# GEGLU feed-forward on one core: one down product of the first group as two row tiles of 64

## The chip, the cores and the metric

The kernel runs on one core of a Trainium2 chip. The metric is the device time of one execution in microseconds. All times in this text are microseconds (us) unless marked ns. The engines are called PE (matrix multiply; PEld is its weight load), DVE (vector), ACT (scalar), POOL and SP (here only a queue that issues transfers).

## What is computed

```python
def reference(x, w_gate, w_up, w_down):
    return (_gelu(x @ w_gate) * (x @ w_up)) @ w_down
```

x is 2048 x 1024, w_gate and w_up are 1024 x 3584, w_down is 3584 x 1024, all bf16; `_gelu` is the tanh form. The change lies in the last product, by w_down.

## The kernel before

The 2048 rows of x are taken in two halves of 1024 (`h`). For each half the hidden activations `hT` (3584 features on partitions, 28 blocks of 128, by 1024 rows) are made first, in `pair_quads`; then two calls of `down_group` multiply them by w_down, 512 rows each (`grp` 0 and 1). The run of the program is thus: hidden for half 0, down groups 0 and 1, hidden for half 1, down groups 2 and 3. `n` numbers the four groups; the change is in group 0, which runs from 183 to 227 us of the profiled span.

A down group is one 2 x 2 block product in Strassen's form as Winograd has it, with seven products in place of eight. The 28 blocks of features are split into two halves of 14 (`NS`), the 512 rows into two halves of 256 and the 1024 output columns into two halves of 512 (`DN`). The seven products are called m1, m5, m6, m7, m2, m3 and m4, in the order in which they run. Each is a sum over 14 blocks `i` of 128 features, for two sets `u` of 128 rows: 28 matmuls of 128 x 128 (weights) by 128 x 512 (moving), which add up in two PSUM banks, one for each `u`. m1 and m2 have bf16 operands. The other five have sums and differences of blocks as operands, held in fp32r (4 bytes): the left ones (`s1` to `s4`, `a22`) in `s_mem`, made by `s_down`, mostly on DVE; the right ones (`t1` to `t4`, `b22`) in `t_mem`, made by `t_down`: t1 and t3 on DVE, b22 by a cast on ACT, t2 and t4 by a transfer on SP from `t_dram`, where an earlier stage put them. The profile shows fp32r matmuls as f32.

`t_mem` is a ring of 20 slots (`NR`) for operands of 14 blocks each, so the next operand's first six blocks are made ahead, and its blocks 6 to 13 go into slots that the present product has read. `s_mem` has two places for a left operand; s1, s2 and s4 share the first, a22 and s3 the second. Hence work is put behind a product's matmuls: the argument `behind` of `product` is called after each odd `i`, and what it emits waits for that matmul. For m3 (left operand s4, right operand b22, banks 4 and 5, called QB) that is `behind_m3`: after i = 1, 3, 5 and 7 a transfer of two blocks of t4, which m4 reads from its seventh block on; after each odd i two blocks of s1 of the next group on DVE; and after i = 9, 11 and 13 two blocks of t1 of the next group on DVE. m4 runs in the order `tail`: i = 0 to 8 with both u in turn, then i = 9 to 13 for u = 0, then for u = 1.

Each engine's instructions run in the order in which they are emitted (`on` ties each to the one before). `evacuate` copies finished banks into `o_sb` on ACT, `store` issues their transfers on SP.

QB holds a part sum before m3: m6 and an added m5 have been put there by ACT and DVE, and m3 adds to it (`start` is false). `m_pool` has one buffer for each of the two m5 tiles, which hold the m5 product in SBUF.

Of the kernel before, what the change touches and what calls it, by code (L numbers as in the profile page):

```python
# [11 lines left out]
F32 = mybir.dt.float32  # L12
# [22 lines left out]
def kernel(  # L35
# [8 lines left out]
    nc = tc.nc  # L44
    P = 128
# [7 lines left out]
    TB = 512  # L53
# [15 lines left out]
    NS = KF // 2  # L69
# [15 lines left out]
    m_pool = ctx.enter_context(tc.tile_pool(name="m5", bufs=1))  # L85
# [20 lines left out]
    banks = [psum.tile([P, TB], F32, name=f"bank{i}") for i in range(8)]  # L106
    PB, VB, QB, RB = (0, 1), (2, 3), (4, 5), (6, 7)
    last_on = {}

    def on(engine, inst):  # L110

        if engine in last_on:
            tc.add_manual_dep(
                inst.ins, last_on[engine].ins.name, SCHED_DEP, reason="engine order"
            )
        last_on[engine] = inst
        return inst
# [7 lines left out]
    def dve(inst):  # L125
        return on("dve", inst)
# [12 lines left out]
    def pe(inst):  # L139
        return on("pe", inst)  # L140
# [431 lines left out]
    def right(grp, name, i0, i1):  # L572

        r0 = ((grp * len(SEQ) + SEQ.index(name)) * NS + i0) % NR
        assert r0 + i1 - i0 <= NR
        t = t_mem[:, r0 * DN : (r0 + i1 - i0) * DN]
        return t.rearrange("p (a b) -> p a b", b=DN)

    def left(n, i0, i1):
        s0 = (n * NS + i0) * 2 * P  # L580
        return s_mem[:, s0 : s0 + (i1 - i0) * 2 * P].rearrange(
            "p (a b) -> p a b", b=2 * P
        )
# [97 lines left out]
    def down_group(hT, h, grp, then):  # L681
# [3 lines left out]
        n = h * NGRP + grp  # L685
# [5 lines left out]
        plain = [(i, u) for i in range(NS) for u in range(2)]  # L691
# [2 lines left out]
        head = [(i, u) for u in range(2) for i in range(5)]  # L694
        head += [p for p in plain if p[0] >= 5]

        def product(name, bset, lhs, rhs, start, stop, behind=None, order=plain):

            left_of = [0] * NS
            for i, u, *part in order:  # L700
                bank, c0, c1 = part or (bset[u], 0, DN)
                pe(
                    nc.tensor.matmul(  # L703
                        banks[bank][:, c0:c1],
                        lhsT=lhs(i, u),
                        rhs=rhs(i)[:, c0:c1],
                        start=start and i == 0,
                        stop=stop and i == NS - 1,
                        skip_group_check=True,
                    )  # L710
                )
                left_of[i] += 1
                if behind is not None and left_of[i] == 2 and i % 2 == 1:
                    behind(i - 1)
# [8 lines left out]
        def lsum(n):  # L723
            return lambda i, u: left(n, i, i + 1)[:, 0, u * P : (u + 1) * P]
# [6 lines left out]
        def rsum(name):  # L731
            return lambda i: right(grp, name, i, i + 1)[:, 0, :]
# [14 lines left out]
        def evacuate(bset, l, d, halves=False):  # L747

            outs = []
            for u in range(2):  # L750
                if halves and u == 1:
                    r0 = h * SH + t0 + (2 * l + u) * P
                    for bank, c in ((bset[u], 0), (VB[u], DH)):
                        dst = o_pool.tile([P, DN], BF16, name="o_sb")[:, 0:DH]
                        src = banks[bank][:, c : c + DH]
                        if c == 0:
                            dve(nc.vector.tensor_copy(out=dst, in_=src))
                        else:
                            act(nc.scalar.copy(out=dst, in_=src))  # L759
                        c0 = d * DN + c  # L760
                        outs.append((out2[r0 : r0 + P, c0 : c0 + DH], dst))
                    continue
                dst = o_pool.tile([P, DN], BF16, name="o_sb")[:]
                r0 = h * SH + t0 + (2 * l + u) * P
                if last_grp and u == 0:
                    dve(nc.vector.tensor_copy(out=dst, in_=banks[bset[u]][:]))
                else:
                    act(nc.scalar.copy(out=dst, in_=banks[bset[u]][:]))  # L768
                outs.append((out2[r0 : r0 + P, d * DN : (d + 1) * DN], dst))
            return outs  # L770

        def store(outs):
            for dst, src in outs:
                sp(nc.sync.dma_start(out=dst, in_=src))

        def store_last(dst, src):
            act(nc.scalar.dma_start(out=dst, in_=src))

        product("m1", PB, h_block(0, 0), b11, True, False)
        for u in range(2):  # L780
            act(nc.scalar.copy(out=banks[QB[u]][:], in_=banks[PB[u]][:]))
# [12 lines left out]

        late = []
        product("m5", VB, lsum(0), rsum("t1"), True, False, behind_m5)
        for i in late:
            t_down(grp, "t3", i, i + 2)
# [6 lines left out]
        def behind_m6(i):  # L805
# [4 lines left out]
            if i == 4:  # L810
                for q in range(4):
                    load_b21(n, q)

        product("m6", QB, lsum(0), rsum("t2"), False, False, behind_m6, tail)
        s_down(hT, grp, "s4", NT2, NS)
        for u in range(2):
# [28 lines left out]
                if NT2 + i >= NS:  # L845
                    t_down(grp + 1, "t1", NT2 + i - NS, NT2 + i - NS + 2)

        product("m3", QB, lsum(0), rsum("b22"), False, True, behind_m3)
        store(out11 + evacuate(QB, 0, 1))
        done("m3")  # L850

# [10 lines left out]
        else:  # L862
            k = NS - NSPLIT
# [18 lines left out]
    for h in range(NH):  # L882
# [9 lines left out]
        for pair in range(first_pair, NPAIR):  # L892
# [14 lines left out]
            if h == 0 and pair >= PPG:  # L907

                n = [min(4 * (pair - PPG + d), NSTEP) for d in range(3)]
# [16 lines left out]
            if 6 < pair < 11:  # L926
                i = 2 * pair - 8
# [81 lines left out]
        for grp, then in enumerate((then0, then1)):  # L1009
            down_group(hT, h, grp, then)  # L1010
# [30 lines left out]
```

## Time and profile before

| what | value |
|---|---|
| time of three runs, median (lowest, highest) | 539.48 (539.43, 539.60) |
| span of the profiled execution | 538.0 |
| what lies around the span, median less span | 1.48 |
| m2 of group 0, 28 bf16 matmuls | 208.4 to 214.4 |
| m3 of group 0, 28 f32 matmuls | 214.4 to 220.8 |
| m4 of group 0, 28 f32 matmuls | 220.8 to 227.2 |
| f32 weight load, 128 x 128, as shown | 0.188 |
| f32 matmul, 128 x 512, as shown (start to modelled end) | 0.389 |
| DVE step of s1 in m3's stretch | 0.69 each |
| DVE step of t1 | 1.22 each |

The span runs from the first to the last instruction of the program on its one core; the time has launch and end around it as well. Matmuls are pipelined: one is shown 0.39 long, but the next starts after some 0.23, so a stage's length is read from the starts. All the first group's stages lie back to back on PE. Weight loads have a row of their own and lie beneath the matmuls.

### The profile page before, as it was taken

The page shows a single profiled execution, that of the slowest core. Times are in us where ns is not written, and L with a number is a line of the kernel's source. Part 1 is how long each engine was busy: PE and PEld are TensorE (multiplying, and loading weights), DVE is VectorE, ACT ScalarE, POOL GpSimd, SP SyncE. Part 2 cuts the span into 40 slices and gives each one's busy share as a digit, 9 for nine tenths or more (in the row PEclk, how much of TensorE's full clock was granted, in tenths as well). Part 3 has the DMA queues.
Part 4 walks back from the last instruction along what each step waited for, and adds up shares of the span by engine and source line. Part 5 has one row for each costly group of instructions (what it writes and reads, how often), then busy time and mean ns, then how long its engine had stood idle before and what let it go on. Part 6 is the DMA issues. An engine that isn't in the chain of part 4 may idle for free.

```text
span 538.0 us, 7084 instructions
## 1 busy us (share of the span) xinstructions
PE 532.4 (99%) x2352; PEld 377.9 (70%) x2388; DVE 364.2 (68%) x476; ACT 263.5 (49%) x447; POOL 244.4 (45%) x212
## 2 busy tenths in 40 slices
PE   9999999999999999999999999999999999999997
PEld 4577776666776686777776677777777766866866
DVE  1988777788775997989574334444444469969861
ACT  2555555555555329117465555555555552462280
POOL 0699877777776000000056776666777730000000
PEclk9999999999999999999999999999999999999999
DMA  9946876785815977789950405041322448677846
GB/s 205 323 128 195 207 252 185 238 262 197 291 61 200 361 239 246 237 279 308 324 171 1 156 1 158 15 142 57 100 78 80 155 133 284 220 246 252 293 141 212
DMA packets 92547, 102.70 MB, mean 191 GB/s; under 512 B 18656, under 2 KB 67424, under 8 KB 92512
## 3 DMA queue, kind: packets, MB, share of 16 engines
q1 hardware_dynamic: 69568, 80.23, 46.0%
q10 hardware_dynamic: 22944, 22.02, 13.4%
q8 instruction: 19, 0.31, 0.2%
q14 instruction: 16, 0.13, 0.1%
HBM read 85.98 MB, written 12.58 MB: 183 GB/s over the span
## 4 chain that ended last, share of the span: by engine, by line
PE 99%; issue 0%; ACT 0%; ACTq 0%
PE bank L413 63%; PE bank L703 33%; PE bank L264 3%; PE bank L202 1%; PE bank L308 0%; ACT bank L468 0%; ACT o_sb L759 0%; ACTq L468 0%
## 5 line engine op out<-in xcount | busy, mean ns | idle before, releaser
L413 PE MATMUL bank<-t_mem,s_mem 128*128 128x512 f32 x1056 | 249.6, 394 | 0.0
L413 PEld LDWEIGHTS bank<-t_mem,s_mem 128*128 128x128 f32 x1056 | 198.1, 188 | 44.1 <-DVE bank L436 0.4
L385 POOL TENSOR_TENSOR s_mem<-w_mem 128x512 fp32r<-128x512 bf16 x102 | 120.3, 1201 | 190.7 <-DVE t_mem L259 102.8
L703 PE MATMUL bank<-t_mem,s_mem 128*128 128x512 f32 (+1 forms) x548 | 127.2, 391 | 0.0
L288 DVE TENSOR_TENSOR hT<-w_mem,bank 128x512 bf16<-128x512 f32 x104 | 71.3, 687 | 79.9 <-PE bank L413 45.7
L703 PEld LDWEIGHTS bank<-t_mem,s_mem 128*128 128x128 f32 x548 | 102.4, 188 | 22.1 <-issue 0.2
L436 DVE TENSOR_TENSOR bank<-bank,m 128x512 f32<-128x512 f32 x108 | 69.9, 694 | 45.2 <-ACT m L458 43.7
L413 PE MATMUL bank<-xT,w_mem 128*128 128x512 bf16 x405 | 96.5, 380 | 1.4
L283 ACT ACTIVATE w_mem<-bank 128x512 f32<-128x512 f32 x104 | 61.8, 596 | 52.9 <-DVE bank L436 35.8
L413 PEld LDWEIGHTS <-w_mem 128*128 128x128 bf16 x432 | 40.2, 98 | 51.6 <-issue 6.8
L385 POOL TENSOR_TENSOR s_mem<-w_mem,s_mem 128x512 fp32r<-128x512 bf16 x52 | 65.8, 1285 | 0.0
L605 DVE TENSOR_TENSOR t_mem<-w_mem 128x1024 fp32r<-128x1024 bf16 x56 | 65.6, 1219 | 0.0
L385 POOL TENSOR_TENSOR s_mem<-s_mem,w_mem 128x512 fp32r<-128x512 f32 x52 | 60.9, 1192 | 0.0
L464 ACT COPY bank<-bank 128x512 f32<-128x512 f32 x54 | 30.8, 570 | 38.9 <-PE bank L413 38.9
L398 ACT CAST s_mem<-w_mem 128x512 fp32r<-128x512 bf16 x54 | 33.1, 615 | 30.6 <-PE bank L413 29.1
L675 DVE TENSOR_TENSOR s_mem<-hT 128x512 fp32r<-128x512 bf16 x52 | 34.2, 686 | 10.2 <-PE bank L703 9.4
L458 ACT COPY m<-bank 128x512 f32<-128x512 f32 x54 | 31.8, 589 | 17.5 <-PE bank L413 17.5
L703 PEld LDWEIGHTS <-hT 128*128 128x128 bf16 x224 | 21.3, 98 | 26.6 <-issue 2.1
L468 ACT COPY bank<-bank 128x512 f32<-128x512 f32 x54 | 30.7, 570 | 12.7 <-PE bank L413 12.7
L630 DVE TENSOR_TENSOR o_sb<-wd_sb,o_sb 128x512 fp32r<-128x512 bf16 x28 | 31.5, 1126 | 0.5
L768 ACT CAST o_sb<-bank 128x512 bf16<-128x512 f32 x27 | 14.8, 585 | 33.9 <-PE bank L703 33.9
L602 ACT CAST t_mem<-w_mem 128x1024 fp32r<-128x1024 bf16 x28 | 26.9, 1048 | 0.0
(45 smaller groups left out, 238.6 us busy)
## 6 DMA issues: line engine op xcount, KB each, us to landing
t_mem<-t_dram SPq DMA_DIRECT2D x56, 512.0 KB, 5.2
w_mem<-in_w_gate_dram ACTq DMA_DIRECT2D x10, 1024.0 KB, 5.5
w_mem<-in_w_up_dram ACTq DMA_DIRECT2D x10, 1024.0 KB, 5.5
wd_sb<-in_w_down_dram SPq DMA_DIRECT2D x28, 256.0 KB, 4.5
t_dram<-o_sb SPq DMA_DIRECT2D x28, 256.0 KB, 2.4
wd_sb<-in_w_down_dram SPq DMA_DIRECT2D x12, 512.0 KB, 7.7
w_mem<-in_w_down_dram SPq DMA_DIRECT2D x4, 1024.0 KB, 6.6
w_mem<-in_w_down_dram SPq DMA_DIRECT2D x8, 512.0 KB, 8.3
```

The lines of the kernel that those rows point to most:

```text
L283: act(nc.scalar.activation(out=g_sb, in_=ps[:], func=ACT.Gelu_apprx_tanh))
L288: nc.vector.tensor_tensor(out=hT[:, fc, tb * TB : (tb + 1) * TB], in0=g_sb, in1=ps[:], op=ALU.mult,)
L385: pool(nc.gpsimd.tensor_tensor(out=t, in0=in0, in1=in1, op=op))
L398: act(nc.scalar.copy(out=t, in_=a(1, 1)))
L413: nc.tensor.matmul(banks[bank][:], lhsT=lhs[:, c, :], rhs=rhs[:, c, :], start=start and c == 0, stop=c == KH - 1, skip_group_check=True,)
L436: nc.vector.tensor_tensor(out=banks[dst][:], in0=banks[src][:], in1=m5[j][:], op=ALU.add)
L458: act(nc.scalar.copy(out=m5[j][:], in_=banks[V_[j]][:]))
L464: act(nc.scalar.copy(out=banks[RB[j]][:], in_=banks[QB[j]][:]))
L605: dve(nc.vector.tensor_tensor(out=t, in0=in0, in1=in1, op=ALU.subtract))
L630: dve(nc.vector.tensor_tensor(out=t, in0=in0, in1=in1, op=ALU.subtract))
L675: dve(nc.vector.tensor_tensor(out=t, in0=in0, in1=in1, op=op))
L703: nc.tensor.matmul(banks[bank][:, c0:c1], lhsT=lhs(i, u), rhs=rhs(i)[:, c0:c1], start=start and i == 0, stop=stop and i == NS - 1, skip_gr ...
```

## The change

In the first group (`n == 0`) m3 is given `rows=True`, and `product` then takes another path. It goes over all 14 blocks twice (`k` = 0, 1). Each matmul takes only 64 of the 128 partitions of its two operands, all 128 weight columns and all 512 moving columns. In the first pass u = 0 takes partitions 0 to 63 and adds to bank 4, and u = 1 takes partitions 64 to 127 and adds to bank 5; in the second pass they change places. So 56 matmuls stand in place of 28, in turn on the lower and the upper half of the array's rows, never two neighbours on one bank, and together they add the same products.

Between the passes DVE copies two columns of each bank into an m5 tile that nothing reads. Since the copy reads what the first pass wrote and comes before what the second pass writes, the second pass's first matmul on a bank waits for that bank's copy, and the copy for the bank's last matmul of the first pass. The steps of `behind_m3` are emitted in the second pass only. The stages before and after m3, and m3 in the other three groups, are as they were. Engine by engine, PE has 28 matmuls and 28 weight loads more, DVE two copies more, just ahead of the first s1 step; the order on ACT, POOL and SP is the same.

```diff
-        def product(name, bset, lhs, rhs, start, stop, behind=None, order=plain):
+        def product(
+            name, bset, lhs, rhs, start, stop, behind=None, order=plain, rows=False
+        ):
 
             left_of = [0] * NS
+            if rows:
+                R2 = P // 2
+                for k in range(2):
+                    for u in range(2):
+                        if k == 1:
+                            seen = m_pool.tile([P, TB], F32, name=f"m5_{u}")
+                            dve(
+                                nc.vector.tensor_copy(
+                                    out=seen[:, 0:2], in_=banks[bset[u]][:, 0:2]
+                                )
+                            )
+                    for i in range(NS):
+                        for u in range(2):
+                            r = slice(((u + k) % 2) * R2, ((u + k) % 2 + 1) * R2)
+                            mm = pe(
+                                nc.tensor.matmul(
+                                    banks[bset[u]][:],
+                                    lhsT=lhs(i, u)[r],
+                                    rhs=rhs(i)[r],
+                                    start=start and i == 0 and k == 0,
+                                    stop=stop and i == NS - 1 and k == 1,
+                                    skip_group_check=True,
+                                )
+                            )
+                        if behind is not None and k == 1 and i % 2 == 1:
+                            behind(i - 1)
+                return
             for i, u, *part in order:
...
-        product("m3", QB, lsum(0), rsum("b22"), False, True, behind_m3)
+        product(
+            "m3", QB, lsum(0), rsum("b22"), False, True, behind_m3, rows=n == 0
+        )
```

## The prediction

> **What bounds the kernel now.** I read the page's share table and chain first, then the same stretch by stages, then the timeline of the product itself, and last the DMA issues and the few rows that price a wait.
>
> ```profile
> span 538.0 us, 7084 instructions
> PE 532.4 (99%) x2352; PEld 377.9 (70%) x2388; DVE 364.2 (68%) x476; ACT 263.5 (49%) x447; POOL 244.4 (45%) x212
> ...
> PE 99%; issue 0%; ACT 0%; ACTq 0%
> ```
>
> PE is busy for 99% of the span and is 99% of the chain: what PE loses anywhere is lost at the end, and work on other engines costs only where PE comes to wait for it. The whole answer is therefore how long PE takes from the first matmul of M3 to the first of M1 in the next group. Stages M7, M2, M3, M4 by windows (length, PE, PEld, DVE, ACT, POOL, clock, DMA share, GB/s):
>
> ```profile
> 201.90:208.40 6.50, 6.50 (x31) 5.19 (x29) 6.50 (x9) 6.16 (x7) 0.00 (x0) 1.00 0.38 124
> 208.40:214.40 6.00, 5.95 (x29) 2.82 (x29) 3.35 (x6) 5.65 (x11) 0.00 (x0) 1.00 1.03 368
> 214.40:220.80 6.40, 6.40 (x29) 5.28 (x29) 4.34 (x6) 1.07 (x2) 0.00 (x0) 1.00 0.91 305
> 220.80:227.20 6.40, 6.40 (x29) 5.00 (x28) 6.40 (x8) 1.66 (x3) 0.00 (x0) 1.00 0.61 211
> ```
>
> M3 is the third row. PE has no hole in it, the granted clock is 1.00, and the DMA engines are 91% busy, which matters below. Now the timeline (start, length, engine, line, operation, count):
>
> ```profile
> 213.58 1.03 PE L703 MATMUL bank<-o_sb,hT 128*128 128x512 bf16 x4
> 214.26 13.12 PE L703 MATMUL bank<-t_mem,s_mem 128*128 128x512 f32 x56
> 227.22 5.14 PE L703 MATMUL bank<-w_mem,hT 128*128 128x512 bf16 x22
> ...
> 533.99 1.11 PE L703 MATMUL bank<-t_mem,s_mem 128*128 128x256 f32 x8
> ```
>
> Four bf16 matmuls take 1.03 and each is shown 0.38 long, so they start (1.03-0.38)/3 = 0.217 apart, the last at 214.23; the first of M3 really streams from 214.45 (its shown start, 214.26, is that of its queueing). M3 and M4 then are 56 matmuls in 227.22-214.45 = 12.77: 0.228 each, 6.39 for M3, and M4 starts at 220.84. The last line is the only f32 row with half the streaming: eight, each shown 0.28 long, so (1.11-0.28)/7 = 0.119 apart.
>
> **The change part by part.** It removes 28 matmuls over 128 rows and adds 56 over 64 rows with the same 512 columns, each with its own weight load. So it can win nothing by arithmetic; it keeps pace only if the two row tiles stream at the same time.
>
> *Pace.* No row shows 64-row tiles. The nearest is the 0.119 row: per matmul one f32 load of 128 columns and half a full stream, just what a tile of an overlapping pair claims. A pair is then 0.238 against 0.228 before, 28 pairs 6.66: +0.27. Lower end: both loads hide, a pair goes at the bf16 pace 0.217: 28 x (0.217-0.228) = -0.31. Upper end, if tiles take turns: 56 x 0.228, +6.39. I take +0.27.
>
> One rule speaks against overlap of another kind. The f32 loads last 0.188 and streams over 0.2, yet full-height matmuls follow at 0.228, so a load overlaps a matmul on the same rows here. The Trainium skill (TensorE: Matmul & The Clock Gate, Part 3, "The mechanism") says that a load overlaps matmuls in flight only where the row group differs. By it a tile would need load plus stream, 0.188+0.217 per pair, and the product +4.96 rather than +0.27; the row of this case decides for me.
>
> *Change of tile height, into and out of M3.* The bf16 to f32 change costs nothing visible (M3's first follows at the bf16 pace), but no row shows a change of tile height. Into M3: from 0 to a full emptying, the shown 0.38 of the last bf16 matmul, a 0.19 load, less the 0.217 that passes anyway: 0.35. I take 0.2. Out: the last matmul must stream for 0.217 where the pair's sum above counted 0.119, 0.10; with emptying, 0.39+0.19-0.12 = 0.46. I take 0.3. Nothing in the rows prefers an end, so these lie in the middle. The Trainium skill (TensorEngine Tiling (Array Packing), "Key Properties") says that a change of tiling mode drains the engine. By that both would go to their upper ends, 0.31 more than I take.
>
> *The half-way wait.* Between the halves VectorE copies two columns of each bank, each copy behind that bank's last matmul of half one, and the first matmuls of half two wait for the copies. Nothing lies ahead of them on DVE, which is idle for 3.82 before its first M3 step:
>
> ```profile
> 215.58 0.69 DVE L675 TENSOR_TENSOR s_mem<-hT 128x512 fp32r<-128x512 bf16 x1 [3.82 <-PE bank L703]
> ...
> L766 DVE CAST o_sb<-bank x4: 681/692/692, 518.2 to 534.2; 128x512 bf16<-128x512 f32 x4
> L757 DVE CAST o_sb<-bank x1: 415/415/415, 534.8 to 534.8; 128x256 bf16<-128x256 f32 x1
> ...
> 4.46 0.29 DVE L316 COPY xT<-bank 128x256 bf16<-128x256 bf16 x1
> ...
> 4.85 0.60 PE L264 MATMUL bank<-xT,w_mem 128*128 128x512 bf16 x1
> ```
>
> That first step waits for M3's fourth matmul, which starts at 214.45+3x0.228 = 215.13, so from a matmul's start to its reader is 0.45. PSUM copies of 512 and 256 columns take 0.692 and 0.415: 1.08 ns a column, so two columns cost 0.14. A copy that ended at 4.75 let PE begin at 4.85: 0.10. Then the f32 load, 0.19, which can't run ahead, as the wait is the matmul's. Sum 0.88, less the 0.24 after which that bank's next matmul would have come: 0.64; the second bank adds 0.01. I take 0.65. Lower: the load does run ahead, 0.45. Upper: both copies last 0.29, the shortest PSUM copy seen: 0.45+0.29+0.29+0.10+0.19-0.36 = 0.96.
>
> *What hangs behind M3.* POOL has no step here. Each step behind an odd i now waits for half two. On SP these are four 512 KB loads of t4 for i = 6 to 13, which M4 reads; on DVE s1 and t1 of the next group.
>
> ```profile
> 215.57 3.10 SPq L600 DMA_DIRECT2D t_mem<-t_dram  x4
> 218.77 3.54 SPq L774 DMA_DIRECT2D out_dram<-o_sb  x4
> 226.50 1.40 SPq L600 DMA_DIRECT2D t_mem<-t_dram  x3
> ...
> DMA to landing us min/median/max: 7.1/7.1/7.1
> ```
>
> The last line is of the fourth load alone, issued at 218.31: it lands at 225.4. M4's matmuls run to i = 8 in pairs, then bank by bank, so i = 12 is first read by the 22nd, at 220.84+21x0.228 = 225.63. Only 0.2 is spare already. After the change half two starts at 214.45+0.2+28x0.119+0.65 = 218.63, its fourth matmul 0.36 later, the first load is issued at 219.43, 3.9 later than before, while M4 starts only 1.4 later. The four then issue as fast as SP does, 0.49 apart as the three at 226.50. Those three landed 3.7, 4.6 and 5.4 after issue, the third 6.4 after the first issue; one more at its spacing of 1.3 is 7.7: 227.1. The four issued at 234.40 landed the last 9.2 after the first (237.1+6.4): 228.6. Need: 222.26+4.79 = 227.05. Late by 0.1 to 1.6; I take 0.5, nearer to the three, whose issue is as dense. The stores behind them on SP have no reader, and the next t2 loads follow M4.
>
> DVE starts its chain at 219.4 instead of 215.58; before it ended at 233.28 with four holes of 0.21 to 0.24 between its s1 steps, now 16.8 without holes end at 236.2. t1, the part that M5 reads, is ready by 232, M5 starts at 235; the first s2 step comes due at 236.3. Hidden, by M1's 6.07; without that cover M5 would wait some 0.5. ACT's casts of b22 end at 209.45, before M3, so half one may read all of them early.
>
> Sum: 0.27+0.2+0.3+0.65+0.5 = 1.9, PE has no slack later that gives it back. The profiled span goes from 538.0 to 539.9; the runs lie 1.48 above the span (539.48), so 541.4.
>
> **The rivals.** *Tiles take turns* (the change doesn't do what it says): for it, no row shows two matmuls streaming at once; against it, 0.119 spacing with loads of 0.19 shows that PE keeps several operations in flight. 6.39+0.2+0.65+0.2, and no late load, since half two then lasts 6.4: +7.4, 546.9. *Loads take turns*: each pair needs two loads one after the other, 0.376; 28 x 0.148 = 4.14, with 1.15 around it +5.3, 544.8. Against it: in the 0.119 row loads shown 0.19 long overlap each other. *Not slower*: at the load's place in each pair, the 0.011 by which f32 trails bf16 hides behind the other tile, -0.31, and with free switches (0 and 0.10), the wait at 0.45 and t4 in time it is +0.24, 539.7. It decides as soon as wait, switches and late load together stay under 1.08+0.31; for it only that each low end is possible, against it that all must come at once. Getting faster by over 0.2% would need -1.08, for which no row has a source.
>
> **How the numbers follow.** A change under 0.2% (1.08 us) can't be told from none. Overlap as summed 0.70; its own range is 540.4 (pace 0.27 kept, the rest at 0, 0.10, 0.45 and 0.1: 0.92) to 543.1 (all upper ends, 0.27+0.35+0.46+0.96+1.6 = 3.64); not slower 0.12; loads in turn 0.08; tiles in turn 0.10. Predicted 541.4, range 540.0 to 545.5, which leaves out the turns and some of the not-slower case. Faster 0.02, same 0.13 (with the lowest corner of the likeliest), slower 0.85.
>
> **What would show it.** In the profile after: the 56 matmuls shown with 64 rows, some 0.12 apart (0.23 if they take turns, 0.19 if loads do); one hole of about 0.65 in the middle with DVE's two small copies in it; M4's first about 1.4 later than 220.84; a hole before M4's 22nd, ended by a t4 landing near 227.5; the rest of the span shifted alike. A shift that grows in later groups, or an M3 under 6.4, would make this wrong.

## The result, and the profile after

| | before | changed |
|---|---|---|
| time of three runs, median (lowest, highest) | 539.48 (539.43, 539.60) | 542.07 (541.85, 544.82) |
| span of the profiled execution | 538.0 | 540.1 |

The ratio is 1.0059, with a 95% interval of 1.0043 to 1.0074: slower, by somewhat more than was forecast (541.4, in a range of 540.0 to 545.5). The medians differ by 2.6, 0.48%; one of the three runs, 544.82, has a span of only 541.1. The profiled execution took 541.85, 1.8 more than its span.

The page of the changed kernel, its share table and the shares of its chain:

```profile
span 540.1 us, 7175 instructions
...
PE 535.0 (99%) x2416; PEld 377.6 (70%) x2416; DVE 363.9 (67%) x478; ACT 263.5 (49%) x447; POOL 244.0 (45%) x212
...
PE 96%; DMA 2%; SPq 1%; issue 0%; ACT 0%; DVE 0%
```

PE's share is still 99%, but the chain is no longer PE's alone: DMA and its queue now hold 3% of it. The stages M2, M3 and M4 by windows (length, PE, PEld, DVE, ACT, POOL, clock, DMA share, GB/s):

```profile
208.10:214.10 6.00, 6.00 (x29) 2.65 (x28) 3.35 (x6) 5.65 (x11) 0.00 (x0) 1.00 1.04 373
214.10:221.50 7.40, 7.15 (x58) 5.73 (x57) 2.93 (x7) 1.07 (x2) 0.00 (x0) 1.00 0.43 136
221.50:229.10 7.60, 6.68 (x29) 4.98 (x28) 7.60 (x9) 1.66 (x3) 0.00 (x0) 1.00 0.85 296
```

M2 is as long as before. M3 has grown from 6.4 to 7.4 with 0.25 of idle PE in it, M4 from 6.4 to 7.6 with 0.92. The clock is 1.00 throughout. The DMA share in M3 has fallen from 0.91 to 0.43: the transfers that filled it run later now, in good part in M4, whose share has risen from 0.61 to 0.85. The timeline, a row for each merged stretch (start, length, engine, line, operation, count, idle time before it and who ended that):

```profile
213.28 1.03 PE L732 MATMUL bank<-o_sb,hT 128*128 128x512 bf16 x4
...
214.23 3.48 PE L717 MATMUL bank<-t_mem,s_mem 64*128 64x512 f32 x28
217.75 0.24 DVE L709 COPY m<-bank 128x2 f32<-128x2 f32 x2 [6.30 <-PE bank L717]
...
217.97 3.12 PEld L717 LDWEIGHTS bank<-t_mem,s_mem 64*128 64x128 f32 x28 [0.67 <-DVE m L709]
217.97 3.54 PE L717 MATMUL bank<-t_mem,s_mem 64*128 64x512 f32 x28 [0.25 <-DVE m L709]
218.80 1.92 SPq L600 DMA_DIRECT2D t_mem<-t_dram  x4
...
221.44 5.05 PE L732 MATMUL bank<-t_mem,s_mem 128*128 128x512 f32 x21
...
227.41 1.85 PE L732 MATMUL bank<-t_mem,s_mem 128*128 128x512 f32 x7 [0.92 <-DMA t_mem<-t_dram]
...
229.11 6.22 PE L732 MATMUL bank<-w_mem,hT 128*128 128x512 bf16 x28
```

Three things are to be seen. The first 28 half-height matmuls take 3.48, about half of the 6.66 that 28 full-height ones are shown to take (M4 of e1 below): the tiles do run in pairs. Between the passes stand the two DVE copies and an idle PE, whose next weight load waits for the first copy. And M4 stops behind its 21st matmul until a t4 load lands.

One number serves from here on: the distance from the last start in M2 to the first start in M1 of the next group. M2's last four are 0.38 long each and take 1.03 in all, so here the last starts at 213.28+0.65 = 213.93, and the distance is 229.11-213.93 = 15.18. Before it was 227.22-214.23 = 12.99. All of the change's loss in the span (2.1) is in these 2.19. The times of the runs differ by more: 2.6 by the medians, 2.3 to 4.0 by the interval of the ratio. Some 0.3 of this gap comes from the profile before. In the later runs, which have each their own span on record, the time lies 1.76 to 1.82 above the span (medians by kernel). By that the span of 538.0 belongs to a run of about 539.8 (an estimate), 0.3 above the median of the three.

The parts of the 2.19, from single starts in the trace (when an f32 matmul begins to stream, the load for the next one goes out, which gives its real start): into M3 0.20 (first stream at 214.34 instead of 214.14); the 28 pairs at 0.228 to 0.230, together as long as 28 full-height matmuls, 0.0; the hole half way 0.52 (last pair at 217.33, next stream at 218.07, 0.23 would have passed anyway); out of M3 0.27; M4's hole 1.18 from start to start (the 0.92 above counts from the shown end). The first four make M4 begin 1.0 later, seen from M2's last start.

### The profile page after: what moved, and what is told of

Read it like the earlier page. It is cut to its first block, busy times and chain, and to the rows that moved or that the text cites. A ratio compares the mean times of both kernels' runs of the same rounds, so it can differ in the third digit from the quotient of the medians.

```text
span 540.1 us, 7175 instructions
## 1 busy us (share of the span) xinstructions
PE 535.0 (99%) x2416; PEld 377.6 (70%) x2416; DVE 363.9 (67%) x478; ACT 263.5 (49%) x447; POOL 244.0 (45%) x212
## 4 chain that ended last, share of the span: by engine, by line
PE 96%; DMA 2%; SPq 1%; issue 0%; ACT 0%; DVE 0%
PE bank L413 63%; PE bank L732 31%; PE bank L264 2%; DMA t_mem<-t_dram 1%; PE bank L717 1%; DMA xT<-in_x_dram 1%; SPq L171 0%; SPq L160 0%; SPq L166 0%; ACT o_sb L788 0%; DVE m L709 0%
## 5 line engine op out<-in xcount | busy, mean ns | idle before, releaser
L413 PEld LDWEIGHTS bank<-t_mem,s_mem 128*128 128x128 f32 x1056 | 198.1, 188 | 44.0 <-DVE bank L436 0.3
L732 PE MATMUL bank<-t_mem,s_mem 128*128 128x512 f32 (+1 forms) x520 | 121.2, 391 | 0.9 <-DMA t_mem<-t_dram 0.9
L732 PEld LDWEIGHTS bank<-t_mem,s_mem 128*128 128x128 f32 x520 | 96.9, 188 | 22.7 <-issue 1.7
L413 PE MATMUL bank<-xT,w_mem 128*128 128x512 bf16 x432 | 97.9, 380 | 0.0
```

What stands on the lines that cost most here:

```text
L413: nc.tensor.matmul(banks[bank][:], lhsT=lhs[:, c, :], rhs=rhs[:, c, :], start=start and c == 0, stop=c == KH - 1, skip_group_check=True,)
L732: nc.tensor.matmul(banks[bank][:, c0:c1], lhsT=lhs(i, u), rhs=rhs(i)[:, c0:c1], start=start and i == 0, stop=stop and i == NS - 1, skip_gr ...
```

## The experiments

All kernels compute the whole product. Distances are from each run's profile; times are compared with runs of the kernel before on the same chip.

| label | distance | over before (12.99) | ratio of times (95%) |
|---|---|---|---|
| e1_four_banks | 13.40 | 0.41 | 1.0019 (1.0011 to 1.0028) |
| e2_wait_alone | 13.27 | 0.28 | 1.0008 (0.9998 to 1.0018) |
| e3_one_tile_in_a_row | 19.53 | 6.54 | 1.0131 (1.0118 to 1.0145) |
| e4_m4_plain | 14.18 | 1.19 | 1.0029 (1.0018 to 1.0041) |
| e5_two_swaps | 14.56 | 1.57 | 1.0032 (1.0020 to 1.0044) |
| e6_all_groups | 15.17 | 2.18 | 1.0217 (1.0201 to 1.0232) |
| e7_changed_again | 15.08 | 2.09 | 1.0051 (1.0039 to 1.0063) |
| e8_late_loads | 13.99 | 1.00 | 1.0022 (1.0013 to 1.0030) |
| e9_four_switches | 13.85 | 0.86 | 1.0029 (1.0017 to 1.0042) |
| e10_runs_of_seven | 14.30 | 1.31 | one run, 541.48 |
| e11_runs_of_two | 13.38 | 0.39 | one run, 540.16 |
| e12_before_m4_plain | 12.96 | -0.03 | 1.0003 (0.9994 to 1.0012) |

Each distance is from one execution. The changed kernel's own, taken twice, agree to 0.1 (e7 and the profile after: 15.08 and 15.18, apart by the moment at which a load lands). The times scatter by 1 to 2 from run to run.

**The switches alone: four banks, one pass.** Lower and upper tile of the same block and rows add into two banks, so nothing changes places and the steps behind M3 stay where they were before.

```diff
-                for k in range(2):
...
-                    for i in range(NS):
-                        for u in range(2):
-                            r = slice(((u + k) % 2) * R2, ((u + k) % 2 + 1) * R2)
+                for i in range(NS):
+                    for u in range(2):
+                        for k in range(2):
+                            r = slice(k * R2, (k + 1) * R2)
...
-                                    banks[bset[u]][:],
+                                    banks[(bset, VB)[k][u]][:],
...
+        if n == 0:
+            m5 = []
+            for u in range(2):
+                m5.append(m_pool.tile([P, TB], F32, name=f"m5_{u}"))
+                act(nc.scalar.copy(out=m5[u][:], in_=banks[VB[u]][:]))
+            for u in range(2):
+                add_m5(QB[u], QB[u], u)
```

> The same 56 matmuls over 64 rows, but in one pass: for each block and set of rows the lower and the upper row tile run as a pair into two banks (4 and 2, then 5 and 3), so nothing changes places half way, and the steps behind M3 stand where they stood before the change; ACT and DVE add the two banks of a set afterwards. Theory (tiles overlap at the old pace; the loss is the two switches of tile height 0.2 + 0.2, the half-way wait 0.5 and the late t4 load 1.2): only the switches are left, M3 lasts 6.39 + 0.4 = 6.8, M4 has no hole, the time is 539.9, 0.4 over before. Rival (row tiles themselves are slow, and the wait and the late load only stand in their shadow): M3 lasts 7.4 here too and the time stays 1 or more over before.

PE's timeline of this kernel:

```profile
213.55 1.03 PE L724 MATMUL bank<-o_sb,hT 128*128 128x512 bf16 x4
214.51 6.66 PE L709 MATMUL bank<-t_mem,s_mem 64*128 64x512 f32 x56
221.09 6.66 PE L724 MATMUL bank<-t_mem,s_mem 128*128 128x512 f32 x28
227.60 1.69 PE L724 MATMUL bank<-w_mem,hT 128*128 128x512 bf16 x7
```

56 half-height matmuls take as long as the 28 of M4 below them, 6.66, and nothing is idle. The distance is 0.41 over before, as the theory said: the 64-row tiles are not slow. The time came out higher than that, 541.02 against 539.94. The traces show most of the rest, at the end of the program. The last store there, from issue to landing, in the kernel before and then in this one:

```profile
DMA to landing us min/median/max: 1.6/1.6/1.6
```

```profile
DMA to landing us min/median/max: 2.3/2.3/2.3
```

In all four kernels with four banks (e1, e9, e10, e11) this store takes 2.1 to 2.3, in the ten others 1.6 or 1.7, and from the last matmul's start to the end of the span pass 3.6 to 3.75 instead of 3.2. Why it lands later is not shown. The profiled execution, the slowest of the eleven, has besides a loss in the *second* group, untouched by the edit: its distance is 13.85 and not 12.96, and its M4 waits 0.6 for its own t4 load.

**The wait alone.** The kernel before, with the two copies behind the first block of M3.

```diff
                 left_of[i] += 1
+                if name == "m3" and n == 0 and (i, u) == (0, 1):
+                    for v in range(2):
+                        seen = m_pool.tile([P, TB], F32, name=f"m5_{v}")
+                        dve(
+                            nc.vector.tensor_copy(
+                                out=seen[:, 0:2], in_=banks[bset[v]][:, 0:2]
+                            )
+                        )
```

> The kernel before with M3 over all 128 rows, and only the half-way wait put in, behind the first block: DVE copies two columns of banks 4 and 5, and the next matmuls on them wait. Theory: the wait costs the same whatever the tile height, 0.50 to 0.65; t4 still comes in time, as the wait stands ahead of all steps behind M3 and shifts them and M4 alike; the time is 540.0 to 540.1. Rival (the wait is dear only because a change of row tile on one bank goes with it): under 0.3, since the full-height matmul's weight load can run ahead.

It costs 0.28, about half. The rival named the number, but not for its reason. The chain is the same in both kernels: 0.42 from the matmul's start to the copy, 0.16 for the copy, 0.05 to the weight load, 0.11 more until the matmul streams, 0.74 to 0.75 in all; the load did not run ahead in either. At full height a bank's turn comes again after two matmuls, 0.46, so 0.29 stays open. In pairs both banks' last matmuls start together and their next turn comes after one pair, 0.23, so 0.52 does. The pairing makes the wait dearer, not the tile height.

**One tile in a row.** The loops over blocks and row sets exchanged, 14 matmuls on one tile, then 14 on the other.

```diff
-                    for i in range(NS):
-                        for u in range(2):
+                    for u in range(2):
+                        for i in range(NS):
...
-                        if behind is not None and k == 1 and i % 2 == 1:
+                            if behind is not None and k + u == 2 and i % 2 == 1:
```

> The changed kernel with the loops over blocks and row sets exchanged: in each pass 14 matmuls on one row tile and one bank, then 14 on the other, so that neighbours never stand on different tiles except at the change. Theory (pairs share the array at the same time, each matmul still streams for its full 512 columns): no overlap is left, M3 grows by 28 x 0.228 = 6.4 over the changed kernel, the time is 548.2 to 548.5, with the late load as in the changed kernel, since the steps stand behind the last 14. Rival (a 64-row matmul is simply twice as fast, pair or no pair): M3 lasts 7.4 as in the changed kernel and the time stays near 542.

PE's timeline of this kernel; the row in the middle is a part of the stretch above it, asked for by itself:

```profile
214.93 11.50 PE L717 MATMUL bank<-t_mem,s_mem 64*128 64x512 f32 x56
...
216.66 1.76 PE L717 MATMUL bank<-t_mem,s_mem 64*128 64x512 f32 x10
...
232.46 1.85 PE L732 MATMUL bank<-t_mem,s_mem 128*128 128x512 f32 x7 [0.99 <-DMA t_mem<-t_dram]
```

A half-height matmul alone takes a full step: the starts within a run lie 0.23 apart. So it is the pairing that pays for the doubled count. But M3 grew by 4.2 over the changed kernel and not by 6.4. The wait half way is gone, since a bank is read again only 14 matmuls after its copy (0.5). And where the two tiles meet, PE does not keep the order of the program: ten matmuls in 1.76, the last of them shown 0.38 long, start within 1.38, in which a step of 0.23 allows seven. The first tile's eleventh starts at 217.35, the other tile's first is shown from 217.36 and streams from 217.46, and the two go on side by side until the first tile is through, three steps later. Which matmul is which, DVE tells: its copy of the first tile's bank waits for that tile's fourteenth matmul.

```profile
218.45 0.16 DVE L709 COPY m<-bank 128x2 f32<-128x2 f32 x1 [6.31 <-PE bank L717]
```

That is 0.42 behind the start at 218.03, the same 0.42 as in the changed kernel, and the matmul at 218.03 is the 17th by start. Two such meetings save nearly 0.8 each.

**The late load, from M4's side.** The changed kernel, with M4 of the first group in plain order.

```diff
-            product("m4", RB, lsum(1), rsum("t4"), False, True, behind_m4, tail)
+            product("m4", RB, lsum(1), rsum("t4"), False, True, behind_m4, plain if n == 0 else tail)
```

> The changed kernel, and in addition M4 of the first group runs its blocks in plain order, both row sets in turn to the end, so blocks 10 and 12 are read at its 21st and 25th matmul and not at its 20th and 22nd. Theory (the hole in M4 ends when the fourth t4 load lands, 5.7 after M4's start): the need moves 3 x 0.228 = 0.68 later, the hole shrinks from 1.16 to 0.5, the time falls by 0.7 against the changed kernel, to 541.3. Rival (the hole comes from DVE's later s1 and t1 steps or from the banks, and the load only happens to land then): the hole stays at 1.1 to 1.2, or moves and keeps its length.

The distance fell by 1.0, and the hole to 0.2, which is also what the waits list for PE on this transfer. The hole shrinks with the moment at which the block is read, as the theory has it; a little more than forecast, as the last load landed 5.4 after M4's start this time and not 5.7.

**The late load, from M3's side.** The kernel before, with the four t4 loads emitted together behind block 7 and the first held until M3's 15th matmul.

```diff
-            if NT2 + i < NS:
+            if n == 0:
+                if i == 6:
+                    late_dep.append(m3_mm[14])
+                    for q in (0, 2, 4, 6):
+                        t_down(grp, "t4", NT2 + q, NT2 + q + 2)
+            elif NT2 + i < NS:
                 t_down(grp, "t4", NT2 + i, NT2 + i + 2)
```

> The kernel before, M3 over all 128 rows in one pass, but the four t4 loads of blocks 6 to 13 are held until M3's 15th matmul, so that the first leaves 2.75 ahead of M4's start, as in the changed kernel. Theory (the hole in M4 is the late load and nothing else): M3 lasts 6.39 as before, M4 gets a hole of 1.1 to 1.2 ahead of its 22nd matmul, the distance from M2 to M1 is 14.15, the time is 1.2 over before. Rival (in the changed kernel DVE's later chain or the denser M3 has a part in it): the hole is under 0.6.

PE's timeline of this kernel:

```profile
213.90 11.51 PE L709 MATMUL bank<-t_mem,s_mem 128*128 128x512 f32 x49
226.18 1.84 PE L709 MATMUL bank<-t_mem,s_mem 128*128 128x512 f32 x7 [0.78 <-DMA t_mem<-t_dram]
227.86 1.47 PE L709 MATMUL bank<-w_mem,hT 128*128 128x512 bf16 x5
```

28 matmuls of M3 and 21 of M4 run without a gap, then PE waits for the transfer: the same hole at the same matmul, with no row tile in the kernel. By the real starts it is 1.0 long, and the distance is 1.00 over before, a little short of the theory's 1.1: the four landed 8.3 after the first left, against 8.5 in the changed kernel.

**Two swaps, loads early.** M3 cut at block 8; blocks 0 to 7 are through with both passes early, at the price of a second wait.

```diff
+                H = 8
+                for k, j0, wait, free in (
+                    (0, 0, False, False),
+                    (1, 0, True, True),
+                    (1, H, False, False),
+                    (0, H, True, True),
+                ):
```

> The changed kernel with M3 cut at block 8: the banks change places behind block 7 of the first part (blocks 0 to 7, both halves of the rows), the second part (blocks 8 to 13) begins on the side where the first ended and changes places once more. So there are two half-way waits, but blocks 1, 3, 5 and 7 are done with early and the four t4 loads can leave some 4.3 ahead of M4 and not 2.75. Theory (late load 1.18, one wait 0.52): no hole in M4, a second hole of 0.5 in M3; from the last start of M2 to the first of M1 of the next group 14.5, against 15.18 in the changed kernel and 12.99 before; the time is 1.5 over before and 0.66 under the changed kernel. Rival (loads take as long as the engines of the transfers are busy, whenever they leave): the hole in M4 stays near 1 and the distance grows to 15.7.

```profile
214.21 2.11 PE L723 MATMUL bank<-t_mem,s_mem 64*128 64x512 f32 x16
216.57 3.56 PE L723 MATMUL bank<-t_mem,s_mem 64*128 64x512 f32 x28 [0.25 <-DVE m L715]
220.29 1.75 PE L723 MATMUL bank<-t_mem,s_mem 64*128 64x512 f32 x12 [0.15 <-DVE m L715]
221.97 6.64 PE L738 MATMUL bank<-t_mem,s_mem 128*128 128x512 f32 x28
```

PE's timeline shows two holes in M3 and none in M4 (28 in 6.64). 14.56 was forecast as 14.5: a load that leaves 1.4 earlier is in time (217.40 instead of 218.80), and buying that with one more wait pays: the distance is 0.62 shorter.

**The change in all four groups.**

```diff
-            "m3", QB, lsum(0), rsum("b22"), False, True, behind_m3, rows=n == 0
+            "m3", QB, lsum(0), rsum("b22"), False, True, behind_m3, rows=True
```

> The change in all four groups and not in the first alone. Theory (switches 0.2 and 0.27, wait 0.52, late load about 1.2 wherever t4 follows as closely): each group pays some 2.1, the time is 8 to 8.5 over before. Rival (the late load is a matter of the first group alone, where transfers of x run at the same time): 4.0 for the four products and 1.2 once, 5.2 over before.

The span grew by 10.4 and the time by 12.1. By group the stretch from M2's last start on grew by 2.2, 4.1, 2.1 and 1.8. Both theories missed the second group. DVE's timeline there, and then what PE waited for in this kernel (total, times, longest):

```profile
263.26 0.69 DVE L383 TENSOR_TENSOR wd_sb<-w_mem 128x512 fp32r<-128x512 bf16 x1 [5.86 <-DMA w_mem<-in_w_up_dram]
263.87 1.29 DVE L383 TENSOR_TENSOR wd_sb<-wd_sb,w_mem 128x512 fp32r<-128x512 f32 x2
265.07 1.29 DVE L383 TENSOR_TENSOR wd_sb<-w_mem 128x512 fp32r<-128x512 bf16 x2
266.28 0.22 DVE L709 COPY m<-bank 128x2 f32<-128x2 f32 x2
```

```profile
PE bank L717 <- DVE m L709: 2.8, 4, 2.1
PE bank L732 <- DMA t_mem<-t_dram: 2.8, 4, 0.9
```

In that group five steps that prepare the next half, held up by a transfer of weights until 263.26, stand ahead of the copies, and the half-way wait lasts 2.1 and not 0.25. The late load comes in all four groups (four waits, 0.5 to 0.9).

**The changed kernel again**, without an edit.

> The changed kernel once more, beside the others on one chip: by the sum of its stages 2.1 to 2.2 over before. Rival (the first comparison was luck of the chip): under 1.5 or over 3.

542.55 against 539.67, ratio 1.0051; distance 2.09 over before, M4's hole 0.81 as the profile counts it. The loss repeats. The times' difference, 2.9, is again above that of the stages. It lies inside the span (medians 540.75 against 537.9), but the profiled execution, with 540.3, shows only a part of it.

**Four switches.** The four-bank form, blocks 5 to 9 at full height in the middle of M3.

```diff
-                        for k in range(2):
-                            r = slice(k * R2, (k + 1) * R2)
+                        whole = 5 <= i < 10
+                        for k in range(1 if whole else 2):
+                            r = slice(0, P) if whole else slice(k * R2, (k + 1) * R2)
```

> The four-bank form of M3, with blocks 5 to 9 over all 128 rows between row tiles before and after: the tile height changes four times in place of twice, with fewer row tiles. Theory (each change of height costs PE 0.20, the pairs nothing): from the last start of M2 to the first of M1 13.8, that is 0.8 over before; time 0.8 over before. Rival (the 0.41 of the four-bank form is spread over its 28 pairs): 18 of 28 pairs remain, 13.25, 0.26 over before.

13.85: 0.86 for four switches, 0.41 for two. The cost is of the switch, some 0.21 each, and not of the pairs.

**How far PE looks ahead.** The four-bank form with runs of seven, and of two, on each tile in turn.

```diff
+                seq = [
+                    (i, u, k)
+                    for j0 in (0, 7)
+                    for u in range(2)
+                    for k in range(2)
+                    for i in range(j0, j0 + 7)
+                ]
```

and for the runs of two

```diff
+                seq = [
+                    (i, u, k)
+                    for i in range(NS)
+                    for k in range(2)
+                    for u in range(2)
+                ]
```

> The four-bank form of M3, with the pairs pulled apart: seven matmuls in a row on the lower tile, then seven on the upper, eight runs in all. Theory (PE lets the other tile's matmuls start some three ahead of their turn, as seen where the tiles met in the run of fourteen, and no further): seven meetings save 3 each, 56-21 = 35 steps of 0.228, M3 8.0 plus the switches 0.4, that is 8.4; M4 then has late t4 loads as well. Rival (no looking ahead, the tiles overlap only as neighbours): 56-7 = 49 steps, M3 11.2 plus 0.4. Other rival (any distance will do): 6.8.

> The four-bank form of M3, with two matmuls in a row on the lower tile, then two on the upper. Theory (PE looks some three ahead): overlap stays whole, M3 lasts 6.8, M2 to M1 13.4, as in turn. Rival (only neighbours overlap): one of two pairs is lost, 42 steps, 9.6 plus 0.4.

PE's timelines, of the runs of seven and then of the runs of two:

```profile
214.23 7.54 PE L714 MATMUL bank<-t_mem,s_mem 64*128 64x512 f32 x56
```

```profile
213.83 6.65 PE L713 MATMUL bank<-t_mem,s_mem 64*128 64x512 f32 x56
```

Runs of two lose nothing. Runs of seven lose 0.9, where I expected 1.6 and the strict rival 4.8. The starts show why: the second tile comes in beside the first tile's fourth matmul (215.03), ahead of three that stand before it, and from there on each tile finds its next run in time, so that little more than the beginning and the end runs alone.

**Time to spare, in the kernel before.** M4 of the first three groups in plain order.

```diff
-            product("m4", RB, lsum(1), rsum("t4"), False, True, behind_m4, tail)
+            product("m4", RB, lsum(1), rsum("t4"), False, True, behind_m4, plain)
```

> The kernel before, with M4 in plain order in the first three groups, so that the last t4 load has 0.68 more time. In the profile of the kernel before it has 0.2 to spare in the first group, and in two of the runs above M4 of the second group shows a hole of 0.4 to 0.9 at this load. Theory (such holes come and go from run to run and lift the mean): the time falls by 0.1 to 0.3, and no M4 has a hole. Rival (they are rare, or the order's other end, banks that are finished later, costs as much): no difference that can be told.

No difference that can be told (539.88 against 539.59). Taking the narrow margin at this load away gains nothing that these runs can tell (0.06% at most by the interval). No version here beats the kernel before.

## Why the prediction was right, point by point

- *Do the tiles overlap?* Taken as the likeliest; shown. Pairs start 0.003 apart and follow each other at 0.228, and in the run of fourteen single tiles need a full step each. Both rivals in which tiles or loads take turns fall.
- *Pace, +0.27 forecast, 0.0 measured.* This term was mis-sized. I took the matmuls of half the columns as the nearest row, 0.119 each, and doubled them. Those carry some 0.011 each over half the bf16 pace (0.119 against 0.108). I counted that piece twice for a pair; it shows once, as at full height (0.228 against 0.217). Why was not tried. The lower end (pairs at the bf16 pace) was not reached, so the not-slower rival had nothing to live on. The Trainium skill's rule that a load overlaps matmuls only of other row groups (TensorE: Matmul & The Clock Gate, Part 3, "The mechanism") would have made a pair 0.405 long, estimated from this case's load and bf16 pace; 0.228 was measured, so the row was the better guide.
- *Switches, 0.2 and 0.3 forecast, 0.20 and 0.27 measured* (0.2 of the latter without the half-way wait, which leaves the two tiles 0.08 out of step). The skill's rule that a change of tiling mode drains the engine (TensorEngine Tiling (Array Packing), "Key Properties") agrees in kind: there is a cost each time. In size the cost is somewhat over half of a full emptying by the shown ends, 0.35 and 0.46; whether PE empties is not shown.
- *Half-way wait, 0.65 forecast, 0.52 measured.* The chain was right; two links were too long: 0.05 and not 0.10 from the copy to PE, and 0.11 and not 0.19 from the load to its matmul, which streams before the load is shown as ended. The 0.10 came from a row in which the matmul's load had gone ahead (load 4.64, matmul 4.85); here the load itself waits for the copy. e6 shows the condition under which it holds: nothing ahead of the copies on DVE.
- *Late t4 load, 0.5 forecast, 1.18 measured*, within the stated 0.1 to 1.6. The place, the matmul and the cause were right; the size was under half. My 0.5 puts the landing of the last load 8.1 after the first issue, between the 7.7 from three loads as densely issued and the 9.2 of four others; it took 8.5 (e5, where the load left earlier, 8.1). And PE's wait stands ahead of the weight load, so the stream begins 0.18 after the landing (227.31 and 227.49), which I left out.
- *DVE's later chain costs nothing*: right. M1 and M5 of the next group follow without a gap.
- The sum was 1.9 and is 2.1 to 2.2: the errors of pace and wait (-0.27 and -0.13) and of the load (+0.68) partly cancel. That the total came out nearer than its largest term is luck.
- *From span to time, 1.48 added*: too little. It set a median against the span of another execution; with the 1.8 of the later runs the same sum gives 541.7.

The times of e1, e7 and e9 lie 0.6 to 0.8 further above before than their first group explains. In the profiled executions of e1 and e9 the late last store accounts for 0.6 and 0.5. Still open are why that store lands later, the 0.8 of e7, and why M4 of the second group has holes at its t4 load in some profiles (e1, e4) and none in others.

## What to carry to other kernels

Row tiles of 64 that run in pairs on two banks win nothing where the contraction fills the array: in this case (f32, 512 columns) a pair costs what the one full-height matmul did, and each change of tile height costs PE about 0.2. What decides is what the rearrangement does to the work behind it: two passes over the operands free every slot half a product later, and a load with 0.2 to spare became the largest part of the loss. If tiles must be used, give each its own bank, so that one pass suffices and nothing has to wait half way.

## What the runs showed of the hardware that was not expected

PE's matmuls on different row tiles do not keep the order of the program among each other: in the run of fourteen the other tile's first is shown from 217.36 and streams from 217.46, ahead of three that stand before it (217.58, 217.80, 218.03), while each tile keeps its own order. In the run of fourteen and in the runs of seven alike the other tile came in ahead of three; tiles overlap fully in runs of two and nearly so in runs of seven.

With the change in all four groups, three of four runs had a mean granted clock of 0.997 and spans of 550.0 to 550.9, and the one with 1.000 had 548.4. Idle stretches of up to 2.1 on PE are new in that kernel; that they let the clock drop was not tried.
